# Attention and gated feed-forward for one decoded token: fetch blocks, semaphore numbers and the last wait at the end of the program

## The chip, the cores and the metric

The kernel runs on one core of a Trainium2 chip. The metric is the device time of one execution in microseconds (us). Before the change it is 687.66 us, the median of three runs (687.66, 686.55 and 687.93).

A core has five engines, each with a program of its own: TensorE (PE in the profile; its weight loads stand apart as PEld), VectorE (DVE), ScalarE (ACT), GpSimd (POOL) and SyncE (SP). They meet only through semaphores: counters that one engine, or a landing DMA, raises and on which another waits.

## What is computed

One token `x` of 512 numbers is normalised, goes through an attention over a cache of 8192 keys and values for each of 32 heads, and in parallel through a gated feed-forward block whose result gates the attention's:

```
xn = layernorm(x)                                   # [512]
q  = (xn @ wq).reshape(32, 128)                     # wq [512, 4096]
p  = softmax(q . k_cache * 128 ** -0.5)             # k_cache [32, 8192, 128]
o  = p @ v_cache                                    # v_cache [32, 8192, 128]
s  = o.reshape(4096) @ wo                           # wo [4096, 512]
g  = silu((sigmoid(xn @ w_gate) * (xn @ w_up)) @ w_down)
out = x + s * g                                     # [512]
```

All is float32. The two caches are 134 MB each, and the profile counts 293.67 MB read from HBM in all. The output is 2 KB.

## The kernel before, in words

The heads go in 16 pairs. A pair's keys, and its values, are 8 MB each, laid out as 128 partitions with 128 rows of 128 numbers. Three buffers (`slots`) hold such a block: 0 and 1 take the keys of alternate pairs, 2 the values. For each pair DVE multiplies the keys by q (line 408) and sums the products (line 409); ACT takes the exponentials; PE multiplies them into the values. All loads are issued by SP, in one queue, in an order written out by hand, each behind the step that frees its buffer.

The end of the program is what the change touches. The last matrix, `wo`, comes in ten pieces that shrink to 256 KB (`W_ENDS`; the list `ld_o` holds what each raises, `ld_o[-1]` is the last). DVE and PE share its rows; `fold` adds the parts together over the partitions; line 541 multiplies by the gate and line 543 adds `x`. SP waits for that last sum (`wait(SP, t)`) and sends the output (line 559), which raises the semaphore `s_out` by 16 when it has landed. SP has by then taken 16 from `s_out` (line 557) which ACT gave at the start.

What follows the output's issue is clearing up. The whole program stands inside a loop body that runs once: each engine adds one to a register (line 561) and takes a branch that falls through to the block "done" (line 563). There SP clears the kernel's own semaphores with one instruction (line 571). Leaving the critical section (`section.close()`, recorded under line 105) makes every engine drain and tell SP so; then SP waits for `s_out`, and so for the landing of the output (it, too, is recorded under line 105). At the end of the kernel function (line 598) the framework adds two meetings of all engines: each drains and raises a "gather" semaphore, POOL waits for the four others and releases them. Between the two meetings POOL clears the framework's semaphores, with one drain and one range clear for each unbroken range of numbers.

Before, `s_out` is allocated first and has number 99; the kernel's 41 others are 100 to 140; those that the framework makes for the critical section are 141 to 147.

Of the kernel before, what the change touches and what calls it, by code (L numbers as in the profile page):

```python
# [13 lines left out]
P = 128  # L14
# [37 lines left out]
def kernel(  # L52
# [12 lines left out]
    nc = tc.nc  # L65
# [27 lines left out]
    W_DVE = [r for r in range(W_FOLD) if r not in W_PE]  # L93
    V_CUTS, K_HALF, K_FEW = (NB // 2, NB * 13 // 16), NB // 2, (NB * 3 // 16, NB // 4)

    DVE, ACT, SP, POOL = nc.vector, nc.scalar, nc.sync, nc.gpsimd
    PE = Later(nc.tensor)
    pe_only = OrderedEngineSet([nc.tensor.engine])

    s_out = tc.alloc_semaphore("s_out")
    ACT.nop().then_inc(s_out, 16)
    section = ctx.enter_context(ExitStack())
# [38 lines left out]
    pm, pn = wide[3][:, :4], wide[4][:GP, :Dh]  # L143


    sems = []

    def semaphore(name):
        sems.append(nc.alloc_semaphore(name))
        return sems[-1]  # L150


    class Steps:
        def __init__(self, name):
            self.sem, self.n = semaphore(name), 0
# [9 lines left out]
    def load(eng, name, dst, src, *after):  # L165
        wait(eng, *after)
        if name not in loads:
            loads[name] = [semaphore(f"s_{name}"), 0]
        loads[name][1] += 16
        eng.dma_start(dst, src).then_inc(loads[name][0], 16)  # L170
        return loads[name][0], loads[name][1]

    def wait(eng, *steps):
        for s in steps:
            if s is not None:
                eng.wait_ge(*s)


    turned, spread_m, valued, picked = (semaphore(f"s_{n}") for n in ("turned", "spread", "valued", "picked"))
    maxed, reduced, powers, copied = (semaphore(f"s_{n}") for n in ("maxed", "reduced", "powers", "copied"))  # L180
    added = semaphore("s_added")
# [304 lines left out]
    ld_o = []  # L486
# [66 lines left out]
        PE.play(each)  # L553
    PE.play(after)

    SP.wait_ge(s_out, 16)
    SP.nop().then_inc(s_out, -16)
    wait(SP, t)
# [6 lines left out]
            br.branch_hint(hints[e])  # L565
    body.close()
    nc.switch_bb("done")

    used = sorted(s.num for s in sems)
    assert used == list(range(used[0], used[0] + len(used)))  # L570
    SP.sem_clear(range(used[0], used[-1] + 1))

    section.close()
    SP.wait_ge(s_out, 16)


# [26 lines left out]
```

## Time and profile before

| | us |
|---|---|
| median of three runs | 687.66 |
| the profiled execution's own time | 687.53 |
| its span, first to last instruction | 685.1 |
| DVE busy | 615.2 (90%) |
| PE busy | 225.8 (33%) |
| ACT busy | 44.6 (7%) |
| HBM, mean over the span | 429 GB/s |

The span covers what the program's own instructions take; the execution's own time has 2.43 us more, which the profile does not break down (687.53 less 685.1). Rows of the profile give times from the start of the span. A name with a q behind it (SPq, POOLq) is an engine's sequencer: drains, semaphore instructions, branches and the issue of DMAs stand there, and are not counted as busy. The views that are used below: the chain of waits that ended last; the timeline of instructions; and, for a single line of the kernel, its instructions on each engine with their count, their duration in ns (least, median, most) and the start of the first and the last.

### The profile page before, as it was taken

The numbers are of one execution on the slowest core, as the hardware profiler recorded it, in microseconds if no ns is written. First come the engines' busy times: TensorE is split into PE (matmuls) and PEld (weight loads), VectorE is DVE, ScalarE is ACT, GpSimd is POOL, SyncE is SP. The second block draws the span as 40 slices with busy tenths as digits, with TensorE's granted clock in tenths as the row PEclk, the third lists the DMA queues.
The fourth block names the chain that finished last, engine by engine and source line by source line (L and its number), as shares of the span: only waits on it lengthen the run. The fifth ranks groups of instructions, "written<-read, shape, count | busy, mean of one in ns | idle before, by whom it ended". The sixth has DMA issues, their size and how long they took to land. (4 is left out here: it accounts for less than half of the span.)

```text
span 685.1 us, 3413 instructions
## 1 busy us (share of the span) xinstructions
PE 225.8 (33%) x1370; PEld 62.5 (9%) x1370; DVE 615.2 (90%) x156; ACT 44.6 (7%) x142; POOL 2.6 (0%) x11
## 2 busy tenths in 40 slices
PE   0353024060503206050513305050513334340666
PEld 0120001010100101010100101010100101010110
DVE  3879999999999998998989898998989999999917
ACT  2130010000000101000000100000010101010000
POOL 0000000000000000000000000000000000000000
PEclk9996657575665757575755757575666656575886
DMA  8999999999999999999999999999999999999997
GB/s 367 434 447 452 448 429 429 429 429 429 429 429 429 429 429 440 471 436 429 429 429 429 429 429 429 429 448 467 432 398 445 412 434 453 429 429 429 429 430 305
DMA packets 8128, 293.67 MB, mean 429 GB/s; under 512 B 920, under 2 KB 928, under 8 KB 1856
## 3 DMA queue, kind: packets, MB, share of 16 engines
q1 hardware_dynamic: 8120, 293.67, 99.3%
q10 hardware_dynamic: 8, 0.00, 0.0%
HBM read 293.67 MB, written 0.00 MB: 429 GB/s over the span
## 5 line engine op out<-in xcount | busy, mean ns | idle before, releaser
L408 DVE TENSOR_TENSOR slot<-slot,q_all 128x16384 f32<-128x16384 f32 (+5 forms) x19 | 275.9, 14521 | 20.7 <-DMA slot<-in_A_k_cache_dram 20.7
L409 DVE TENSOR_REDUCE sc<-slot 128x128 f32<-128x16384 f32 (+5 forms) x19 | 276.0, 14525 | 0.7
L38 PE MATMUL psum<-slot,zeros 128*8 128x512 f32 x1024 | 154.9, 764 | 255.0 <-PEq L38 255.0
L38 PEld LDWEIGHTS psum<-slot,zeros 128*8 128x8 f32 x1024 | 31.1, 106 | 365.2 <-issue 365.2
L38 PE MATMUL psum<-ident,mx 128*1 128x128 f32 x32 | 8.7, 372 | 106.1 <-PEq L38 106.0
L430 ACT COPY o<-psum 128x512 f32<-128x512 f32 x16 | 9.4, 586 | 408.0 <-PE psum L38 408.0
L38 PE MATMUL psum<-slot,ones 128*128 (+3 forms) x36 | 15.9, 613 | 23.1 <-PEq L38 17.5
L283 DVE SCALAR_TENSOR_TENSOR slot<-slot,xn 128x1376 f32<-128x1376 f32 (+1 forms) x8 | 18.9, 2360 | 3.0 <-DMA slot<-in_A_wq_dram 2.7
L38 PE MATMUL psum<-o,pick 128*2 128x128 f32 x128 | 16.5, 272 | 12.8 <-PEq L38 12.8
L416 DVE STREAM_TRANSPOSE psum<-psum 32x128 f32<-32x128 f32 x16 | 5.0, 311 | 12.3 <-PE psum L38 12.2
L423 ACT ACTIVATE zeros<-sc,nb 64x128 f32<-64x128 f32 x32 | 12.8, 399 | 0.9
L38 PE MATMUL psum<-slot,o_all 128*1 128x512 f32 (+1 forms) x48 | 11.0, 552 | 5.0 <-DMA slot<-in_A_wo_dram 5.0
L38 PEld LDWEIGHTS psum<-o,pick 128*2 128x2 f32 x128 | 9.9, 84 | 29.6 <-issue 27.2
L421 ACT ACTIVATE nb<-psum 128x2 f32<-128x2 f32 x16 | 2.8, 172 | 148.2 <-PE psum L38 148.2
L38 PEld LDWEIGHTS psum<-ident,mx 128*1 128x1 f32 x32 | 1.8, 80 | 110.1 <-issue 110.1
L38 PE MATMUL psum<-zeros,rs 128*32 128x2 f32 x32 | 3.7, 187 | 23.5 <-PEq L38 23.5
L401 DVE TENSOR_REDUCE mx<-psum 1x2 f32<-1x128 f32 x16 | 4.4, 277 | 7.6 <-PE psum L38 7.4
L38 PE MATMUL psum<-mx,ones 1*128 1x2 f32 x32 | 8.2, 325 | 7.4 <-PEq L38 7.4
L519 DVE SCALAR_TENSOR_TENSOR q_all<-slot,o_all,q_all 128x512 f32<-128x512 f32 x15 | 10.0, 742 | 0.0
L38 PE MATMUL psum<-slot,o 128*1 128x512 f32 x26 | 5.6, 920 | 12.9 <-DMA slot<-in_B_w_down_dram 12.9
L38 PEld LDWEIGHTS psum<-slot,ones 128*128 128x128 f32 (+1 forms) x36 | 6.3, 197 | 32.5 <-issue 24.6
L38 PEld LDWEIGHTS psum<-mx,ones 1*128 1x128 f32 x32 | 7.3, 283 | 14.3 <-issue 14.3
(54 smaller groups left out, 60.4 us busy)
## 6 DMA issues: line engine op xcount, KB each, us to landing
slot<-in_A_v_cache_dram SPq DMA_DIRECT2D x9, 4096.0 KB, 27.6
slot<-in_A_wq_dram SPq DMA_DIRECT2D x2, 4096.0 KB, 16.7
slot<-in_A_k_cache_dram SPq DMA_DIRECT2D x2, 4096.0 KB, 40.6
slot<-in_A_k_cache_dram SPq DMA_DIRECT2D x1, 6656.0 KB, 42.0
slot<-in_A_k_cache_dram SPq DMA_DIRECT2D x1, 6144.0 KB, 42.1
slot<-in_B_w_gate_dram SPq DMA_DIRECT2D x1, 2752.0 KB, 27.4
slot<-in_B_w_up_dram SPq DMA_DIRECT2D x1, 2752.0 KB, 33.5
slot<-in_B_w_down_dram SPq DMA_DIRECT2D x1, 2560.0 KB, 23.9
```

The lines of the kernel that those rows point to most:

```text
L38: ins = getattr(self.engine, name)(*args, **kwargs)
L283: return dve(DVE.scalar_tensor_tensor(y, w[:, k, cols], xn[:, k:k + 1], y, op0=ALU.mult, op1=ALU.add))
L401: DVE.reduce_max(mx[:1, 1:3], pt[0:1, :].rearrange("o (e p) -> o e p", e=2), axis=AX.X).then_inc(reduced, 1)
L408: wait(DVE, dve(DVE.tensor_mul(k[:, j, :], k[:, j, :], qb[:, i:i + 1, :].to_broadcast([P, n, Dh]))))
L409: summed[i] = dve(DVE.reduce_sum(sc[i % 2][:, j], k[:, j, :], axis=AX.X))
L416: turned_out[i] = dve(DVE.transpose(o, pn.rearrange("e (a r) -> e a r", r=WR)))
L421: wait(ACT, act(ACT.mul(nb, pm[:, :2], -SCALE)))
L423: ACT.activation(weights[h, :, e * HT:(e + 1) * HT], sc[i % 2][h].rearrange("p (g b) -> p g b", b=HT), AF.Exp, bias=nb[h, e:e + 1], scale= ...
L430: ACT.copy(o1, po).then_inc(copied, 1)
L519: ins = DVE.scalar_tensor_tensor(part[n], wo_t[:, r, :], col, part[n], op0=ALU.mult, op1=ALU.add)
```

## The change

Three things are changed, all behind the last load.

- **Alignment.** Each engine's program gets an instruction `addr_align`, which puts the instruction behind it at an address that is a multiple of 128 instructions (256 for PE); with `max_nops=0` the gap is jumped over instead of being filled. ACT, DVE, POOL and PE have it at the start of the block "done". SP has it ahead of the output. ACT and POOL first wait for the last landing of `wo` and raise a new semaphore, `s_left`; SP waits for the last landing and for both of them ahead of its own.
- **Semaphore numbers.** The kernel's semaphores, now 42 with `s_left`, are allocated at once and first (99 to 140); `s_out` comes after them and has number 141, next to the framework's: POOL now clears one range, 141 to 147. SP's clear in "done" now covers 99 to 140.
- **The last wait.** ACT, not SP, waits for `s_out` at the end.

```diff
--- before.py
+++ after.py
@@ -93,12 +93,14 @@
+    N_SEMS = 42
     DVE, ACT, SP, POOL = nc.vector, nc.scalar, nc.sync, nc.gpsimd
...
+    sems = [nc.alloc_semaphore(f"s_{i}") for i in range(N_SEMS)]
     s_out = tc.alloc_semaphore("s_out")
     ACT.nop().then_inc(s_out, 16)
@@ -143,11 +145,10 @@
-    sems = []
+    unused = list(sems)
 
     def semaphore(name):
-        sems.append(nc.alloc_semaphore(name))
-        return sems[-1]
+        return unused.pop(0)
@@ -553,6 +554,12 @@
     PE.play(after)
 
+    left = semaphore("s_left")
+    for eng in (ACT, POOL):
+        wait(eng, ld_o[-1])
+        eng.nop().then_inc(left, 1)
+    wait(SP, ld_o[-1], (left, 2))
+    SP.addr_align(P, max_nops=0)
     SP.wait_ge(s_out, 16)
     SP.nop().then_inc(s_out, -16)
     wait(SP, t)
@@ -565,13 +572,16 @@
     nc.switch_bb("done")
+    for eng in (ACT, DVE, POOL):
+        eng.addr_align(P, max_nops=0)
+    PE.engine.addr_align(2 * P, max_nops=0)
 
     used = sorted(s.num for s in sems)
-    assert used == list(range(used[0], used[0] + len(used)))
+    assert not unused and used == list(range(used[0], used[0] + len(used)))
     SP.sem_clear(range(used[0], used[-1] + 1))
 
     section.close()
-    SP.wait_ge(s_out, 16)
+    ACT.wait_ge(s_out, 16)
```

How this stands in the programs is shown at three places. An instruction's waits are in brackets; drains and bare semaphore instructions are not listed, and their waits stand at the next row. The line numbers after the change are its own (566 is the output, 559 before). The first place is the end of SP's program, before:

```order
L170 DMA slot<-in_A_wo_dram 128x512 x4
L230 UNCONDITIONAL_BRANCH
L559 DMA out_dram<-g_row 4x128 [waits s_out,s_dve]
L561 REGISTER_ALU
L563 COMPARE_AND_BRANCH
L571 ISA
L105 UNCONDITIONAL_BRANCH
L105 NO_OP [waits SP_49,PE_sequencer_49,DVE_sequencer_49,Activation_sequencer_49,SP_sequencer_49,s_out,Pool_sequencer_49]
L598 UNCONDITIONAL_BRANCH
```

And the same with the change, where the kernel's semaphores have numbers for names: `s_40` is raised by the last piece of `wo`, `s_41` is `s_left`, and `s_1` is DVE's (`s_dve` before):

```order
L171 DMA slot<-in_A_wo_dram 128x512 x4
L231 UNCONDITIONAL_BRANCH
L562 ISA [waits s_41,s_40]
L566 DMA out_dram<-g_row 4x128 [waits s_out,s_1]
L568 REGISTER_ALU
L570 COMPARE_AND_BRANCH
L581 ISA
L107 UNCONDITIONAL_BRANCH
L107 NO_OP [waits SP_49,DVE_sequencer_49,PE_sequencer_49,SP_sequencer_49,Activation_sequencer_49,Pool_sequencer_49]
L608 UNCONDITIONAL_BRANCH
```

The alignment (L562) stands ahead of the output, behind two waits, and `s_out` has left SP's last row of waits. The second place is the end of ACT's program, before:

```order
L428 COPY den<-psum 32x2 [waits s_added]
L430 COPY o<-psum 128x512 [waits s_valued]
L230 UNCONDITIONAL_BRANCH
L561 REGISTER_ALU
L563 COMPARE_AND_BRANCH
L105 UNCONDITIONAL_BRANCH
L598 UNCONDITIONAL_BRANCH [waits SP_49]
```

And with the change:

```order
L429 COPY den<-psum 32x2 [waits s_12]
L431 COPY o<-psum 128x512 [waits s_6]
L231 UNCONDITIONAL_BRANCH
L568 REGISTER_ALU [waits s_40]
L570 COMPARE_AND_BRANCH
L576 ISA
L107 UNCONDITIONAL_BRANCH
L608 UNCONDITIONAL_BRANCH [waits SP_49,s_out]
```

ACT now waits for the last landing ahead of its branch, has the alignment (L576) at the head of "done", and waits for the output at its end. The third place is the end of POOL's program, before:

```order
L316 MEMSET slot 128x1536 [waits s_q_spread]
L230 UNCONDITIONAL_BRANCH
L561 REGISTER_ALU
L563 COMPARE_AND_BRANCH
L105 UNCONDITIONAL_BRANCH
L598 UNCONDITIONAL_BRANCH [waits SP_49]
L598 ISA [waits barrier_Pool_Activation_PE_DVE_SP_gather]
L598 ISA
```

And with the change:

```order
L317 MEMSET slot 128x1536 [waits s_14]
L231 UNCONDITIONAL_BRANCH
L568 REGISTER_ALU [waits s_40]
L570 COMPARE_AND_BRANCH
L576 ISA
L107 UNCONDITIONAL_BRANCH
L608 UNCONDITIONAL_BRANCH [waits SP_49]
L608 ISA [waits barrier_Pool_Activation_PE_DVE_SP_gather]
```

The two clears behind the gather (L598 ISA) have become one.

## The prediction

> **What bounds the kernel now.** I read the page first, then the chain of waits, then the end of the timeline, and last the sequencers' instructions by line, since what the change touches is not counted as busy.
>
> ```profile
> span 685.1 us, 3413 instructions
> DVE  3879999999999998998989898998989999999917
> DMA  8999999999999999999999999999999999999997
> ```
>
> The DMA engines are at nine tenths or more in all but the first and the last of 40 slices, and DVE nearly so. Nothing in the change adds to the bytes loaded or to DVE's arithmetic, so some 680 of the 685 us should stay as they are. The chain of waits, cut to the end, shows where the load hands over:
>
> ```profile
> 650.73 27.81 DMA slot<-in_A_wo_dram
> 678.58 1.73 PE psum L38 x6
> 680.33 0.70 DVE q_all L494
> 681.08 0.66 PE psum L38 x16
> 681.76 0.30 DVE g_row L541
> 682.08 0.29 DVE g_row L543
> ```
>
> From 680.33 on no load is on the path: it is DVE, PE, DVE, DVE, and 682.37 (682.08 and 0.29) is when the result is there. The timeline has the same stretch with what PE waited for, and the output's issue:
>
> ```profile
> 680.51 0.10 PEld L38 LDWEIGHTS psum<-slot,o_all 128*1 128x1 f32 x8 [0.29 <-DMA slot<-in_A_wo_dram]
> 681.07 0.10 PEld L38 LDWEIGHTS psum<-q_all,ones 128*1 128x1 f32 x8 [0.46 <-DVE q_all L494]
> 681.18 0.21 PEld L38 LDWEIGHTS psum<-slot,o_all 128*1 128x1 f32 x8
> 682.40 0.64 SPq L559 DMA_DIRECT2D out_dram<-g_row  x1
> ```
>
> At 680.51 PE still waits for a piece of wo, the last but one; the rows at 681.18 use the last piece without idle time ahead of them. So the last landing lies between 680.51 and 681.18, and 1.2 us at least are left between it and the output at 682.40. That gap is what the change works in. What follows the output stands under lines 105, 571 and 598:
>
> ```profile
> L105 SPq EVENT_SEMAPHORE  x4: 17/22/368, 683.4 to 683.7; - x4
> L105 ACTq DRAIN  x1: 8/8/8, 683.5 to 683.5; - x1
> L105 DVEq DRAIN  x1: 10/10/10, 683.5 to 683.5; - x1
> L105 SPq NOP  x1: 13/13/13, 684.1 to 684.1; - x1
> ...
> L571 SPq EVENT_SEMAPHORE_RANGE_CLEAR  x1: 101/101/101, 683.3 to 683.3; - x1
> ...
> L598 POOLq DRAIN  x4: 34/50/71, 683.6 to 684.8; - x4
> L598 POOLq EVENT_SEMAPHORE  x4: 17/17/17, 684.3 to 685.0; - x4
> L598 SPq DRAIN  x3: 7/7/7, 684.2 to 684.5; - x3
> L598 ACTq DRAIN  x2: 8/8/8, 683.5 to 684.5; - x2
> L598 POOLq EVENT_SEMAPHORE_RANGE_CLEAR  x2: 48/58/67, 684.5 to 684.7; - x2
> ```
>
> SP's longest semaphore instruction (368 ns, the last, begun at 683.7) is its wait for the output, which so has landed at 684.1, 1.7 us after its issue began. The other engines have drained by 683.6 and stand idle. From 684.1 the path is SP's NOP and two drains (684.2), POOL's gather (684.3), two range clears (684.5 and 684.7), the second meeting (685.0). The tail from 682.37 to 685.1 is 2.7 us, 1.7 of it the output's flight.
>
> The profiled execution took 687.53 us, 0.13 less than the median of 687.66; 2.43 us of it lie outside its span. I work the sum from 687.53 and set the forecast between it and the one from the median.
>
> **The change part by part.**
>
> *Semaphore numbers.* POOL clears one range instead of two. What goes is a clear (67 ns) and a drain (71 ns), 0.14 us busy; from the start of the first clear to that of the second it is 0.2 us. I take -0.17. Between the two meetings POOL alone works and the others wait for its release, so all of it is on the path. SP's own clear takes one number more: 101 ns for 41 is 2.5 ns each, and it ends at 683.4, long before the landing: nothing.
>
> *ACT waits for the output.* SP's NOP and two drains leave the path behind the landing: 684.1 to 684.3, 0.2 us. In their place ACT's wait ends, ACT drains (8 ns) and raises the gather; ACT's two drains at 683.5 stand under 0.1 us apart. I take -0.1, with 0 and -0.2 as bounds. SP does its NOP and drains meanwhile, as the idle engines do now. Behind ACT's wait only its drain is queued, and POOL's gather waits for that.
>
> *The new waits ahead of the alignment.* ACT and POOL wait for the last landing, raise the semaphore, and go on to a branch, the alignment and a drain. Nobody needs that drain before SP has cleared at 683.4, so 2 us cover it; without that cover each waits a few tens of ns more. SP waits for the landing and for both. A handoff between sequencers is under 0.1 us (SP's raise at 683.4, the drains of the others at 683.5), so SP is free at 681.3 at the latest. Behind its wait stands the output, and for that DVE waits for nothing until 682.37: 1.1 us of cover. Before, SP took its 16 from the output's semaphore at 666.9 and sat idle; now these 17 ns come behind the alignment, in the same cover.
>
> ```profile
> L557 SPq EVENT_SEMAPHORE  x1: 17/17/17, 666.9 to 666.9; - x1
> ...
> L548 PEldq COMPARE_BRANCH  x8: 83/215/226, 28.7 to 35.1; - x8
> L551 PEldq COMPARE_BRANCH  x16: 87/223/243, 109.9 to 664.4; - x16
> L563 DVEq COMPARE_BRANCH  x1: 67/67/67, 682.2 to 682.2; - x1
> L563 SPq COMPARE_BRANCH  x1: 45/45/45, 683.2 to 683.2; - x1
> ```
>
> *The five jumps.* The trace of before has no aligned jump. Its nearest rows are PE's loops: a branch taken back is 215 to 243 ns, one that falls through 83 to 87; on the other engines the untaken branch is 45 to 67 ns. So a jump whose target is at hand costs 0.05 us from below and 0.24 from above. ACT, POOL and SP make theirs at about 681.3, PE at 681.4 and DVE at 682.3; the drains that need them start at 683.5. SP has 1.1 us, DVE 1.2, the others 2: nothing on the path. From above a jump costs a transfer of code. The nearest row for a small transfer with idle queues is the output, 1.7 us from issue to landing; with loads in the queues, the token's 2 KB:
>
> ```profile
> 1.48 1.08 ACTq L170 DMA_DIRECT2D x_row<-in_A_x_dram  x1
> 8.32 0.40 DVE L253 STREAM_TRANSPOSE g_row<-x_row 128x128 f32<-128x128 f32 x1 [6.87 <-DMA x_row<-in_A_x_dram]
> ```
>
> That is 6.8 us, but all loads have landed here, so 1.7 is the nearer. From below a jump could also gain, if a stall that now lies in the 2.43 us outside the span moves into the cover; at most those 2.43. I take nothing, since no row of the program's own five engines ahead of 685.1 shows one stopped without a semaphore or a transfer to wait for at its end.
>
> [...]
>
> *The sum.* -0.17 - 0.1 = -0.27 us. From 687.53 that is 687.26, from the median 687.39. I forecast 687.3, span 684.8. That is 0.05% down; this kernel's runs lie 0.2% apart (686.55 to 687.93), so anything within 0.2%, 1.4 us, can't be told from no change.
>
> **The rivals.**
>
> *SP's jump pays for code: slower.* Place: line 562 ahead of the output. If its block comes by a transfer after the jump, the output leaves at 681.3 plus that transfer instead of 682.4. With 1.7 us it leaves at 683.0, 0.6 late: 687.3 + 0.6 = 687.9, not told from no change. With two such transfers in a row, 3.4 us, it leaves at 684.7: 2.3 late, 689.6. At the loaded price of 6.8 it would be 5.7 late, 693.0. It decides from a transfer of 1.1 us on, and passes 0.2% at 1.1 + 1.7 = 2.8 us. DVE's jump at 682.3 has the same cover, but its drain is needed only at POOL's gather (684.3), so SP's is the dearer. For it: SP's program is short and straight, and nothing shows that the next block is there; five engines would ask at once. Against it: all of DVE's and ACT's long programs run to the end without a stop of that kind.
>
> *A stall outside the span goes: faster.* The 2.43 us hold what the profile doesn't itemise. If an engine there stops for one transfer of 1.7 us and the jumps move that ahead, the time is 687.3 - 1.7 = 685.6; if all of it went, 684.9. For it: nothing of these 2.43 us is hidden by work, and each tenth counts. Against it: they must also hold the start and the end of the execution itself. [...]
>
> *The alignment does nothing.* If the next multiple of 128 lies in a block that is loaded anyway, the jump is a branch and no more: the forecast's 687.3. It goes with the forecast.
>
> **How the numbers follow.** The forecast with the idle alignment: 0.58. The paid jump: 0.22, of which 0.06 with one transfer (687.9, within 0.2%) and 0.16 with more. The stall outside: 0.20, of which 0.18 by more than 0.2%. So faster 0.18, same 0.58 + 0.06 + 0.02 = 0.66, slower 0.16. The forecast's own range is 686.5 to 688.2: -0.4 to 0 for its two terms and 0.7 either way for the runs' scatter. The whole range reaches to one transfer gained, 685.6, and to a paid jump of 3.0 us (681.3 + 3.0 is 1.9 late), 689.2; what lies beyond, two transfers or the loaded price, has some 0.1, and more than one transfer gained 0.05.
>
> **What would show it.** Right: the output's issue stays 0.03 us behind line 543's end; one range clear by POOL; ACT's wait, not SP's, ending with the landing; from the landing to the end 0.7 us where it is 1.0 now; the time less the span still 2.4. The paid jump: the issue of the output well behind the end of line 543, with the idle time ahead of it; or DVE's drain later than SP's clear. The stall outside: span near 684.8 and the time less the span clearly under 2.4. The forecast would be wrong, too, if the load's stretch up to 680.5 moved, which nothing here should do.

## The result, and the profile after

| | before | after |
|---|---|---|
| median | 687.42 us (22 runs, 686.55 to 688.29) | 688.67 us (22 runs, 687.86 to 689.75) |
| ratio of after to before | | 1.0016, 95% interval 1.0010 to 1.0022 |
| the profiled execution: its time, its span, time less span | 687.53, 685.1, 2.43 | 688.84, 687.0, 1.84 |
| means over the runs of span and of time less span (for before, over its runs beside the experiments) | 685.2 and 2.4 | 686.86 and 1.80 |

The change makes the kernel slower by 0.16%, 1.25 us by the medians. That is less than the 0.2% that I had set as the bound of what can be told, but the interval lies wholly above 1. Two movements hide in it: the span grew by 1.7 us, and what lies outside it shrank by 0.6.

The load's stretch is as before within the runs' scatter. The end of the timeline of the kernel after (start, duration, engine, line, operation):

```profile
682.01 0.29 DVE L542 TENSOR_TENSOR g_row<-g_row,psum 128x128 f32<-128x128 f32 x1 [0.74 <-PE psum L38]
682.33 0.29 DVE L544 TENSOR_TENSOR g_row<-g_row,x_row 128x128 f32<-128x128 f32 x1
682.65 0.65 SPq L566 DMA_DIRECT2D out_dram<-g_row  x1
```

The last sum starts at 682.33 where it was 682.08, and the output leaves 0.03 us behind its end (682.62), as before. SP's alignment, which stands between its waits and the output, shows under lines 562 and 564 of the kernel after (line, engine, operation, count: ns least/median/most, first and last start):

```profile
L562 SPq COMPARE_BRANCH  x1: 33/33/33, 681.5 to 681.5; - x1
...
L564 SPq EVENT_SEMAPHORE  x1: 17/17/17, 682.0 to 682.0; - x1
```

SP jumps at 681.5 and takes its 16 from `s_out` at 682.0: about 0.45 us, and 0.6 us ahead of the output. It is not SP that is late. The jumps of the four others, under lines 576 and 577, and the first instruction of each behind its jump, under line 107:

```profile
L577 PEldq COMPARE_BRANCH  x1: 4349/4349/4349, 681.7 to 681.7; - x1
...
L576 POOLq COMPARE_BRANCH  x1: 33/33/33, 681.6 to 681.6; - x1
L576 ACTq COMPARE_BRANCH  x1: 44/44/44, 681.6 to 681.6; - x1
L576 DVEq COMPARE_BRANCH  x1: 61/61/61, 682.5 to 682.5; - x1
...
L107 SPq EVENT_SEMAPHORE  x3: 17/28/519, 683.7 to 686.2; - x3
L107 POOLq DRAIN  x1: 41/41/41, 683.7 to 683.7; - x1
L107 ACTq DRAIN  x1: 67/67/67, 684.1 to 684.1; - x1
L107 DVEq DRAIN  x1: 39/39/39, 685.6 to 685.6; - x1
L107 PEldq DRAIN  x1: 68/68/68, 686.1 to 686.1; - x1
```

Before, all four drained at 683.5. Now ACT comes 2.5 us after its jump, DVE 3.1, PE 4.4. Only PE's stall is written into its branch; on ACT and DVE the branch reads 44 and 61 ns and the stall is seen in the late drain alone. What SP waited for in the last 30 us (line, releaser: us in total, times, longest):

```profile
SPq L107 <- PEq L107: 2.2, 1, 2.2
SPq L566 <- DVE g_row L544: 0.6, 1, 0.6
```

SP waits 2.2 us for PE to drain; before, its last wait there was the output's landing. The DMA queues from 681 to 687 us of the kernel after (packets, MB, share of the engines in that window) show what was moved while they stood:

```profile
q8 instruction: 2, 0.03, 3.0%
q14 instruction: 6, 0.05, 2.7%
q1 hardware_dynamic: 11, 0.00, 0.2%
```

The profiled span of before has no row "instruction" at all. Now eight packets of code are moved: two of 16 KB in q8 (PE's, as its alignment alone shows below) and six of 8 KB in q14 (the others'). 16 and 8 KB stand to one another as the 256 and 128 instructions of the alignments. When they start is seen in the same window (40 slices of 0.15 us, busy tenths of the DMA engines):

```profile
DMA  0000000000920000010000001000000000100040
```

Four start in slices 10 and 11 (682.5 to 682.8), about 1.0 us behind the jumps of SP, POOL, ACT and PE, and the fifth in slice 17 (683.6), 1.0 us behind DVE's. PE's is on its way until 684.55, and PE drains 1.5 us later. The last three (slices 24, 34 and 38) start 0.6 to 0.7 us behind the drains of ACT, DVE and PE. By these times SP and POOL have one packet each, ACT, DVE and PE two; the queue doesn't name the engine. SP goes on at 682.0, before any of them starts, so it waited for none.

The last rows, under line 608 of the kernel after, give the output's landing and the end:

```profile
L608 ACTq COMPARE_BRANCH  x1: 33/33/33, 685.1 to 685.1; - x1
L608 POOLq EVENT_SEMAPHORE_RANGE_CLEAR  x1: 73/73/73, 686.7 to 686.7; - x1
```

ACT's branch is where its wait for the output ends: 685.1, 2.45 us after the issue at 682.65, where it was 1.7. One range clear is left, as meant. From the issue of the output to the span's end it is 4.4 us now and was 2.7 before.

### The profile page after: what moved, and what is told of

It reads as the page before. It is cut to its first block, busy times and chain, and to the rows that moved or that the text cites. A ratio compares the mean times of both kernels' runs of the same rounds, so it can differ in the third digit from the quotient of the medians.

```text
span 687.0 us, 3420 instructions
## 1 busy us (share of the span) xinstructions
PE 225.8 (33%) x1370; PEld 62.5 (9%) x1370; DVE 615.3 (90%) x156; ACT 44.6 (6%) x142; POOL 2.6 (0%) x11
```

## The experiments

Nothing of the computation differs between these kernels, only the alignments, their waits and the last wait. "Tail" is from the output's issue to the end of the span in the profiled execution, "landing" from the output's issue to its landing there, "outside" the mean over the runs of time less span. Each median is of 11 or 12 runs; before, measured with them, took 687.45 to 687.61. The theory at the start was that PE's jump is the loss; its rivals were the other jumps, ACT's wait, and a lengthened load.

| | aligned | tail | landing | mean span | outside | ratio to before, 95% interval |
|---|---|---|---|---|---|---|
| before | none | 2.7 | 1.7 | 685.2 | 2.4 | |
| after | all five, at the end | 4.4 | 2.45 | 686.9 | 1.80 | 1.0016 (1.0010 to 1.0022) |
| e1 | none | 2.5 | 1.7 | 685.1 | 2.3 | 0.9996 (0.9988 to 1.0005) |
| e7 | none; SP waits | 2.5 | 1.7 | 685.0 | 2.5 | 0.9997 (0.9988 to 1.0006) |
| e9 | ACT, POOL, SP, at the end | 2.5 | 1.7 | 685.2 | 2.4 | 1.0001 (0.9992 to 1.0009) |
| e6 | DVE, at the end | 3.7 | 2.25 | 686.3 | 2.2 | 1.0010 (1.0001 to 1.0019) |
| e2 | all but PE, at the end | 3.7 | 2.3 | 686.3 | 2.6 | 1.0022 (1.0013 to 1.0030) |
| e3 | PE, at the end | 3.6 | 1.7 | 686.1 | 1.83 | 1.0004 (0.9995 to 1.0012) |
| e8 | all but PE, early | 2.5 | | 685.5 | 2.0 | 0.9997 (0.9988 to 1.0006) |
| e4 | all five, early | 2.5 | | 686.3 | 1.87 | 1.0008 (1.0000 to 1.0017) |
| e5 | PE, ahead of the `wo` rows | 2.5 | | 686.7 | 1.92 | 1.0011 (1.0001 to 1.0022) |
| e11 | the same; SP waits | 2.5 | | 686.6 | 1.82 | 1.0015 (1.0006 to 1.0025) |
| e10 | PE, ahead of the pair loop; SP waits | 2.7 | | 686.5 | 1.74 | 1.0007 (0.9997 to 1.0016) |
| e12 | PE, ahead of its first step; SP waits | 2.5 | | 686.4 | 1.88 | 1.0012 (1.0003 to 1.0021) |

**No alignment (e1).** Of the change, the numbers and ACT's wait are left.

```diff
-    left = semaphore("s_left")
-    for eng in (ACT, POOL):
-        wait(eng, ld_o[-1])
-        eng.nop().then_inc(left, 1)
-    wait(SP, ld_o[-1], (left, 2))
-    SP.addr_align(P, max_nops=0)
...
-    for eng in (ACT, DVE, POOL):
-        eng.addr_align(P, max_nops=0)
-    PE.engine.addr_align(2 * P, max_nops=0)
```

> The changed kernel without any alignment and without the new waits ahead of it; semaphore numbers and ScalarE's last wait stay. Theory A (the jumps alone cost; the other two edits are worth what the prediction said): 0.27 us under before, 687.15 against a median of 687.42, span 684.8, time less span 2.4, output landed 1.7 us after its issue, one range clear by POOL. Theory B (ScalarE's wait or the numbers cost by themselves): not under before.

687.48 us, tail 2.5: the loss is in the alignments and the waits ahead of them (e9, below, has the waits and no loss). The landing to the end, under line 599 of this kernel:

```profile
L599 ACTq DRAIN  x2: 8/8/8, 684.5 to 684.7; - x2
...
L599 ACTq COMPARE_BRANCH  x1: 44/44/44, 684.3 to 684.3; - x1
L599 POOLq EVENT_SEMAPHORE_RANGE_CLEAR  x1: 73/73/73, 684.8 to 684.8; - x1
```

ACT's wait rides on a branch that it takes; its drain comes 0.2 us after the wait has ended. That is as long as SP's NOP and drains took.

**The numbers alone (e7)**, e1 with SP waiting for the output.

```diff
-    ACT.wait_ge(s_out, 16)
+    SP.wait_ge(s_out, 16)
```

> The new semaphore numbers alone: no alignment, and SyncE waits for the output as before. If ScalarE's wait is worth nothing, because it rides on a branch that takes as long as SyncE's NOP and drains: tail from the output's issue 2.5 us, the same as with ScalarE's wait. If it is worth the 0.1 us of the prediction: 2.6.

687.30 us, and a tail of 2.5 again (issue at 681.88, end at 684.4). So the numbers give the 0.2 us of the tail, and it makes no difference which engine waits. In the medians 0.2 us can't be told from nothing.

**All but PE (e2).**

```diff
-    PE.engine.addr_align(2 * P, max_nops=0)
```

> The changed kernel with TensorE's alignment alone left out. Theory A1 (each jump pays for its own code, whatever the others do): VectorE's jump still takes 3.0 us and sets the end, SP's last wait ends at 685.6 instead of 686.2, span 686.4. Theory A2 (the five transfers crowd one another, TensorE's 16 KB above all): ScalarE's and VectorE's jumps take 1.5 us or less, the output lands 1.7 us after its issue, span 685.0. Both: time less span goes back from 1.8 to 2.4 if it was TensorE's alignment that took 0.6 us there, and stays 1.8 if it was another engine's.

688.97 us. Line 107 of this kernel:

```profile
L107 PEldq DRAIN  x1: 8/8/8, 683.3 to 683.3; - x1
L107 ACTq DRAIN  x1: 66/66/66, 684.1 to 684.1; - x1
L107 DVEq DRAIN  x1: 38/38/38, 685.0 to 685.0; - x1
```

With PE's stall gone DVE's is next: its last sum ends at 682.2 and it drains at 685.0. The tail falls only from 4.4 to 3.7. And outside the span all of the gain is lost (2.6 against 1.80), so leaving out the worst jump makes the kernel no faster.

**PE alone (e3)**: e1, with PE's line back.

> The changed kernel with TensorE's alignment alone: none on the other four, and no new waits. Theory A1 (TensorE's jump costs 4.3 us by itself): it still ends at 686.0 and the span is 686.9. Theory A2 (crowding): its jump takes 2.5 us or less, ends by 684.2 and is covered by the output's flight; span 684.9. Time less span: 1.8 if TensorE's alignment is what shortens it, 2.4 if not.

687.91 us. PE's jump under line 569 and its drain under line 107:

```profile
L569 PEldq COMPARE_BRANCH  x1: 3529/3529/3529, 681.5 to 681.5; - x1
...
L107 DVEq DRAIN  x1: 10/10/10, 683.6 to 683.6; - x1
L107 PEldq DRAIN  x1: 68/68/68, 685.1 to 685.1; - x1
```

Alone, PE's jump takes 3.53 us, 0.8 less than beside the others, and the output lands in the old 1.7. The 0.8 us are those of the transfer: its first packet takes 1.13 us here and 1.92 in the kernel after. PE drains 1.5 us behind the rest and the span is 0.9 longer in the mean, but 0.5 comes back outside.

**DVE alone (e6)**, without the new waits.

```diff
-    for eng in (ACT, DVE, POOL):
-        eng.addr_align(P, max_nops=0)
-    PE.engine.addr_align(2 * P, max_nops=0)
+    DVE.addr_align(P, max_nops=0)
```

> VectorE's alignment alone, where the change has it. Theory A1 (each jump waits for its own block, 0.95 us to the transfer's start, 0.3 to 0.6 for 8 KB and 1.4 back): its jump from 682.1 takes 2.6 to 2.8 us and SyncE's wait for it ends at 684.9, the tail from the output's issue is 3.5 us instead of 2.5. The output lands 1.7 us after its issue if it was the crowd of transfers that held it up (2.4 in the change), 2.2 or more if VectorE's one transfer does. Rival (crowding): a jump of 1.5 us or less, hidden; tail 2.5.

688.39 us. The output and line 107 of this kernel, and ACT's branch behind its wait for the output:

```profile
L560 SPq DMA_DIRECT2D out_dram<-g_row x1: 631/631/631, 683.5 to 683.5; - x1
...
L107 ACTq DRAIN  x1: 8/8/8, 684.6 to 684.6; - x1
L107 DVEq DRAIN  x1: 38/38/38, 686.2 to 686.2; - x1
...
L600 ACTq COMPARE_BRANCH  x1: 44/44/44, 685.8 to 685.8; - x1
```

DVE jumps at 683.4 and drains at 686.2: 2.8 us for an 8 KB block, alone. Of its two packets one starts at 684.4, 1.0 us behind the jump, the other behind the landing, at 686.8. With the first beside it the output takes 2.25 us to land (685.8 less 683.54).

**ACT, POOL and SP in place (e9)**, with their waits as in the change.

```diff
-    for eng in (ACT, DVE, POOL):
+    for eng in (ACT, POOL):
         eng.addr_align(P, max_nops=0)
-    PE.engine.addr_align(2 * P, max_nops=0)
```

> The alignments of ScalarE, GpSimd and SyncE where the change has them, with the new waits; none on VectorE and TensorE. Theory A1 (each jump pays about 2.8 us for itself, and only where it has no such cover does it cost): ScalarE's jump from 681.3 ends at 684.1, before the output has landed; SyncE's target is at hand. The output lands 1.7 us after its issue, the tail from the issue is 2.5 us as without any alignment, ratio 0.9998. Rival (any transfer of code there holds up the output): it lands 2.2 us or more after its issue, tail 3.0, ratio 1.0005.

687.39 us: three of the five are free. The code packets in the span of this kernel:

```profile
q14 instruction: 4, 0.03, 0.0%
```

The slices of 0.15 us from 681 to 687 us say whose they are (the last digit, 686.7, is a q8 block behind the span):

```profile
DMA  0000000020110000000000010000000000000030
```

Three start at 682.3, 682.6 and 682.7, 1.0 to 1.3 us behind the jumps of SP (681.3), POOL and ACT (681.4); the fourth starts at 684.6, 0.6 us behind ACT's drain at 684.0. So SP's jump brings a packet too, but SP's stop of about 0.45 us is over before it starts. ACT is back just inside the output's flight (landing at 684.1).

The output, issued at 682.43, lands in the old 1.7 us although code is moved beside it, and so it does in e3 beside PE's 16 KB, which start with it at 682.5. Where it lands late (e6, e2 and the kernel after), DVE's packet starts 0.9 us behind the issue. Why that one holds it up and the others don't is open.

**All early without PE (e8), and with it (e4).** SP's alignment stands behind its last load, ACT's and POOL's behind their last work, DVE's ahead of the last heads; e4 has PE's ahead of the `wo` rows besides.

```diff
     place(0, NG - 1)
+    DVE.addr_align(P, max_nops=0)
     heads_out(NP - 1)
...
+    for eng in (ACT, POOL):
+        eng.addr_align(P, max_nops=0)
     PE.play(before_q)
...
+    PE.engine.addr_align(2 * P, max_nops=0)
     PE.play(after)
+    SP.addr_align(P, max_nops=0)
```

> The early alignments of ScalarE, VectorE, GpSimd and SyncE without TensorE's. Theory C: time less span 2.4 (no gain outside without TensorE's), tail 2.5, ratio 0.9998. If the early jumps on these four themselves slow the load (as the early version's median of 688.0 against an expected 686.6 may say): ratio 1.001 or more, with DVE's last sum later than in the other kernels.

> All five alignments stay, but each stands where its engine idles in the load's last stretch: ScalarE and GpSimd right behind their last work, SyncE behind its last load, VectorE ahead of the last heads (11.9 us idle there), TensorE ahead of its rows of wo (2.6 us idle, then waits for pieces). No new waits. If the jump's price is what was lost and the end's gain of 0.6 us outside the span comes from the alignment itself: span 684.8, time less span 1.8, 686.6 in all, 0.8 under before. Rival: transfers of code under load take far longer (the 2 KB at the start took 6.8 us), TensorE or VectorE are late for wo and the span is 1 us or more over 685.1; or the gain outside the span goes with the place, and time less span is 2.4.

Both tails are 2.5, so the early jumps cost the tail nothing. e8 has four code packets for its four engines. Those at 42.5 and 670.7 us start 3.8 and 3.5 us behind the jumps of POOL (38.7) and SP (667.2). The two others start at 55.3 and 114.3 us, long before DVE (653.0) and ACT (663.8) jump. e8 is even with before (687.33), and e4 only just is not (688.01, interval from 1.0000): what the tail had lost, it lost in the load's stretch.

**PE alone, early (e5, e11, e10, e12).** Since e4's loss came with PE's line, it stands alone here, in three places: from the top of the diff, e12, e10, then e5 and e11. e5 has ACT's wait, the others SP's.

```diff
+    PE.engine.addr_align(2 * P, max_nops=0)
     PE.play(before_q)
...
+    PE.engine.addr_align(2 * P, max_nops=0)
     with nc.Fori(...)
...
+    PE.engine.addr_align(2 * P, max_nops=0)
     PE.play(after)
```

> No alignment but TensorE's, and that ahead of its rows of wo instead of behind them; semaphore numbers and ScalarE's last wait stay, no new waits. Theory C (the alignment of TensorE's program is what takes 0.6 us off outside the span, wherever it stands): time less span 1.8, tail from the output's issue to the end 2.5 us as without alignment, 0.8 under before (ratio 0.9989). Theory D (the gain outside belongs to the paid transfer at the very end, not to the alignment): time less span 2.4 or as without alignment, ratio 0.9998.

> TensorE's alignment alone, ahead of its rows of wo, with the new semaphore numbers and SyncE's last wait. Theory E: ratio 1.0008 or more once more. Theory F: 0.9997 or, with a gain outside the span, 0.9989.

> TensorE's alignment alone, ahead of its loop over the pairs (TensorE has some 20 us of waiting there), new semaphore numbers, SyncE waits for the output. Theory E (an alignment of TensorE's program ahead of the end slows the load's stretch, as the two early versions with a median 0.5 to 0.9 us over before may say): ratio 1.0008 or more, DVE's last sum 1 us or more later. Theory F (those two were scatter from the clock that TensorE was granted early): ratio 0.9997, tail 2.5.

> PE's alignment ahead of PE's first step, where PE waits for the input until 8.7 us and again from 10.8 to 28.5 us, with the semaphore numbers and SP's wait for the output. Nothing of PE's jump, 4.4 us at most, should show on the path. Theory A (an aligned program of PE is what shortens the time outside the span, wherever the alignment stands, and the early kernels lost their gain because the jump split PE's program late): span as in the kernel with the numbers alone, 685.0 in the mean over the runs, 1.8 outside, together 686.8, ratio 0.999. Theory B (the alignment moves PE's later code in its blocks, and that costs the load's stretch 1.1 to 1.5 us as in the early kernels): span 686.2 or more, 1.8 outside, together 688.0 or more, ratio 1.0008 or more. Theory C (only the place of PE's last block counts, and here nothing lands on it): 685.0 and 2.4, ratio 0.9997.

688.50, 687.94, 687.77 and 688.06 us. PE's jump in e5, and in e12 (lines 555 and 548):

```profile
L555 PEldq COMPARE_BRANCH  x1: 186/186/186, 666.8 to 666.8; - x1
```

```profile
L548 PEldq COMPARE_BRANCH  x1: 304/304/304, 1.2 to 1.2; - x1
```

The jump is 0.2 to 0.3 us, less than a tenth of that at the end, and the tail has no loss. All four have the gain outside (1.74 to 1.92), and all four have mean spans 1.2 to 1.5 us longer, all of it ahead of the output, more than they gain. e12 came out as its theory B said: even where the jump falls into PE's idle time at 1.2 us, the span is 686.4. That it is the new place of PE's later code in its blocks which costs this is not shown.

The traces, one execution of each kernel, show where it is lost. The sum of products (line 409 before) that DVE starts at 291.97 us in before starts at 292.8 to 293.1 in e4, e5, e10, e11 and e12, 0.8 to 1.2 us later, and at 292.3 at the latest in every other kernel. In e4, e5 and e10 more is lost near the end, where PE sums the values of the last pair but one. These matmuls in before, and in e4:

```profile
642.14 5.32 PE L38 MATMUL psum<-slot,zeros 128*8 128x512 f32 x32 [4.37 <-PEq L38]
```

```profile
643.31 6.27 PE L38 MATMUL psum<-slot,zeros 128*8 128x512 f32 x32 [3.69 <-PEq L38]
```

From 642 to 650 us PE was granted a clock (1 is full speed) of 0.57 or 0.58 in e4, e5 and e10, of 0.79 in before, e11 and e12, and of 0.66 to 0.84 in the others. ACT copies these sums at 647.5 us in before, at 648.3 in e11, at 648.7 in e12 and at 649.7 in the three. The outputs leave 0.8 (e11), 1.3 (e12) and 2.2 to 3.2 us (the three) later than in before. What causes the first 0.8 to 1.2 us, and why the grant is lower in those three, is open. The granted clock from 28 to 53 us doesn't part the late kernels from the others: PE had 0.86 in e5, e10 and e12 and 0.92 before, but 0.92 in e11 too:

```profile
28.00:53.00 25.00, 15.53 (x28) 6.16 (x28) 20.02 (x23) 8.59 (x20) 1.38 (x1) 0.92 1.05 456
```

(e11's stretch from 28 to 53 us: busy us and instructions of PE, PEld, DVE, ACT and POOL, PE's clock, DMA share, GB/s.)

### The time outside the span

This time is nearly the same in all 22 runs of after, 1.7 to 1.9, and from 1.7 to 3.4 in those of before and of the kernels whose PE has no alignment. The kernels with PE aligned further ahead have 1.7 to 2.2, with one run of 2.5 in e4. The trace goes on for some us behind the span and shows what goes with the longer times. The DMA engines from 685 to 688 us of the kernel before, whose span ends at 685.1 (40 slices of 0.075 us: busy tenths, GB/s; then the packets):

```profile
DMA  0000000000000004000000000700000000000000
GB/s 0 0 0 0 0 0 0 0 0 0 0 0 0 0 0 109 0 0 0 0 0 0 0 0 0 218 0 0 0 0 0 0 0 0 0 0 0 0 0 0
...
q8 instruction: 1, 0.02, 2.0%
q14 instruction: 1, 0.01, 1.1%
```

The same window of e7 (the numbers alone), whose span ends at 684.4:

```profile
DMA  0000003000000000000000700000000000000000
...
q8 instruction: 1, 0.02, 1.9%
```

And of e9 (ACT, POOL and SP aligned), whose span ends at 685.0:

```profile
DMA  0000000000000000000000700000000000000000
```

The digit 7 is a block of PE's code. It begins in slice 25 of before, 686.9 or 1.8 us behind the span; in e7 at 686.7, 2.3 behind; in e9 at 686.7, 1.7 behind. These three profiled executions had 2.43, 2.9 (687.30 less 684.4) and 2.33 us outside their spans (687.33 less 685.0 for e9): in each 0.6 us more than the block's start lies behind the span. In the kernel after nothing starts between 687 and 691 us:

```profile
DMA packets 0, 0.00 MB, mean 0 GB/s; under 512 B 0, under 2 KB 0, under 8 KB 0
```

Its two PE blocks both start inside the span, the second at 686.8. Every other profiled execution, in which no block of PE came over 0.4 us behind the span, had 1.7 to 2.1 outside. So in these executions a block of PE's code that is fetched behind the span goes with 0.3 to 1.2 us more of time there. That the execution waits for it is not shown. Nor can it wait for the block's end: 2.0% of 16 engines' 3 us is 0.96 us, so the block of before is on its way until 2.8 us behind the span, and the 2.43 us outside are over by then, even if all of them lie behind the span. What the runs do show is whose alignment counts: the mean outside is 1.74 to 1.92 in the seven kernels with PE's program aligned, wherever that stands, and 2.0 to 2.6 in the seven without.

## Why the prediction was right or wrong

The forecast was no change, and the time came out 1.4 us above it: outside the forecast's own range of 686.5 to 688.2, inside the whole range up to 689.2. The ratio is inside the 0.2% that I had called no change, but it is a loss, where the sum had said a small gain.

- **Semaphore numbers, -0.17: right.** One clear is left, and e7's tail is 0.2 us under that of before.
- **ACT's wait, -0.1: nothing.** e1 and e7 have the same tail. The drain on which I put the price stood behind a branch taken, 0.2 us.
- **The new waits ahead of the alignment, 0: right.** e9 has them all and a tail of 2.5.
- **The five jumps, 0: the step that failed.** "SP has 1.1 us, DVE 1.2, the others 2: nothing on the path." The covers were right to 0.1 us (from the jumps at 681.5, 681.6, 682.5 and 681.7 to the output at 682.65 and the first drains at 683.7). The price wasn't. PE's early jumps took 0.19 (e4, e5, e11) and 0.30 us (e12), and SP's stop in the kernel after 0.45, over before any packet of code starts; POOL's can't be told, since POOL drains behind SP's clear as it would without a stall. At the end, each with a packet of code starting behind its jump, ACT takes 2.5 to 2.9 us, DVE 2.8 to 3.1 and PE 3.5 to 4.4, against the bound of 1.7 that I had taken from the output's flight. The output was a poor model: it moves 2 KB, and behind its transfer no engine has to start again (PE drains 1.5 us behind the end of its packet). ACT's stall is still hidden, since the output is in flight until 684.1 in e9; DVE's 2.8 with 1.2 us of cover and PE's 3.5 with 2.0 reach beyond that.
- **The output's flight was taken as fixed.** It is 1.7 us without DVE's block, 2.25 beside DVE's alone and 2.45 beside all of them. With all five it doesn't decide (ACT's wait ends at 685.1, PE's drain comes at 686.1).
- **The paid jump as a rival: right mechanism, wrong engine.** I put it at SP, ahead of the output, and called SP's "the dearer". SP goes on at 682.0, and the first packet starts at 682.5; the loss came by the way named in half a sentence ("DVE's drain later than SP's clear"), and most by PE, to which I had given the most cover and the least thought, though its blocks are twice as large by the diff (`2 * P`), and 16 KB against 8 in the trace. ACT, DVE and PE each stand for 2.5 to 4.4 us behind their jumps while code is fetched. I had taken the next aligned block to be at hand, which no row of before shows; for these three it was not. SP waited for none, and POOL is open.
- **A stall outside the span goes, as a rival: the time went, at a third of its price; the stall is not shown.** 0.6 us went, not 1.7, and PE's alignment takes it: e3 has it, e9 and e2 don't, and e6 (2.2) and e8 (2.0) lie between. The trace behind the span of before shows a code fetch, but not that anything waits for it.
- **The load's stretch stays: right** for this change. It doesn't for an alignment of PE further ahead (e4, e5, e10, e11, e12).

The sum by the runs: the span +1.7 (the tail by PE's jump), outside -0.6, together +1.1. The paid jump and the outside stall were worked out as rivals that exclude one another; both kinds of change came at once, and a third of the one was made good by the other. That the time stayed within 0.2% is luck: the forecast had neither the 1.7 us nor the 0.6 in it.

## What to carry to other kernels

At the end of this kernel a jump to a block of code that had to be fetched cost 2.5 to 3.1 us, and PE's 3.5 to 4.4. Price it so, and put it only where the engine has that much to wait for anyway; SP, with its own jump long over, stood 2.2 us for PE's drain, so one engine's cover was not another's. Look for "instruction" rows among the DMA queues, within the span and behind it, and at the first instruction after a jump rather than at the branch's own duration. When a rival says that a cost moves, ask whether it can happen beside the other rivals, not only in their place.

## What was not expected of the hardware

- In e5 the window from 100 to 115 us, with 447 GB/s of loads, has one q8 packet, over 550 us ahead of PE's jump at 666.8 us, and that jump took 0.19 us. That this packet held the jump's target is not shown.
- With one fetch of 8 KB beside it a 2 KB output landed 0.55 us later (e6), with all loads landed; beside the fetches of e9 and e3 it was not later.
- An alignment of PE's code at three different places ahead of its end makes the span 1.1 to 1.5 us longer with no loss in the tail; at the end it costs the load's stretch nothing (e3: the span is longer by what its tail is longer, 0.9). In the traces 0.8 to 1.2 us of it is there by 292 us, and in three of the five, where more is lost near the end, the clock granted from 642 to 650 us was 0.57 or 0.58 against 0.79 in before; no run here shows the cause of either. None of the versions tried is faster than before by more than its interval; e1, e7, e8 and e9 are level with it.
